# A new order of all pieces in a fused retention and channel-mix kernel: first loads, k's queue, the weights' place

## The chip, the cores and the metric

The kernel runs on one core of a Trainium2 chip. Its engines each work through a queue of their own: TensorE (PE; its weight loads are shown as PEld), VectorE (DVE), ScalarE (ACT), GpSimd (POOL) and SyncE (SP). Transfers are issued by SP, ACT or POOL and carried by 16 DMA engines. The metric is the time of one execution in microseconds (us); before the change it is 160.89 us, the median of 3 runs.

## The reference

Two layers follow each other. The first is a retention recurrence over 4 batches, 8 heads, 768 tokens and 64 channels per head:

```python
for t in range(S):
    state = gamma * state + einsum('bhd,bhe->bhde', k[:, :, t], v[:, :, t])
    y[:, :, t] = scale * einsum('bhd,bhde->bhe', q[:, :, t], state)
```

Its output, turned to 4 x 768 rows of 512 channels, goes into a channel mix:

```python
x_prev = x shifted by one token
xk = mu_k * x + (1 - mu_k) * x_prev
xr = mu_r * x + (1 - mu_r) * x_prev
k = maximum(xk @ w_k, 0)            # 512 -> 1024
v = k * k @ w_v                     # 1024 -> 512
out = sigmoid(xr @ w_r) * v         # 512 -> 512
```

## The kernel before

The recurrence is computed in chunks. Tokens are cut into 12 blocks of 256 tokens, three per batch; a block is two chunks (u = 0, 1) of 128. Scores within a chunk, masked by a triangle, give one part of y; the decayed state handed on from chunk to chunk gives the other. Three weights (w_k, w_v, w_r) stay in SBUF as 16-bit floats.

No loop sets the order. A string `ORDER` lists some 610 words, each one piece of work; a loop at the end of the kernel emits them one by one, and every engine executes its own pieces in this order, waiting where a semaphore says so. A word is a code and its arguments, such as `K.2.1` for the second quarter of the keys of block 2. After `@` stand the PSUM banks (0 to 7) that the piece writes. A piece that takes over a bank waits until its last reader is done. The codes:

| code | engine | what |
|---|---|---|
| lq, lk, lv | POOL; SP for k (POOL with `.2` after the block) | load q, k, v of a block; `lk.n.e.j0.j1` and, after the change, `lq.n.j0.j1` load some head pairs only |
| wk, wr, wv | POOL | load a half of w_k, all of w_r, a half of w_v |
| ks | DVE (`.0`) or POOL (`.1`) | scale k by powers of gamma (L188) |
| T, Tk / Tq | PE | turn scaled k: T in 8 transposes of 128 x 128 (L203), Tk in 32 of 64 x 64 (L221) / turn q in 32 (L221) |
| E | ACT | copy a turned q or k out of PSUM (L249) |
| S, M | PE, DVE | scores (L257) of half i, masked (L264) |
| C, U, G | PE, DVE, POOL | k times v of a block (L282), summed to the state (L294, L298), decayed for the next chunk (L301) |
| I, Y | PE | state part and score part of y (L313, L326) |
| D (Du: of one chunk) | DVE | y scaled by powers of gamma into xT (L340, L348) |
| gy | DVE | builds those powers, in eight small steps (L500, L503) |
| dx (du) | DVE (`.0`) or POOL (`.1`) | x minus the x of the token before (L355) |
| X (Xu) | DVE | xk (`X.n.0`) or xr (`X.n.1`) of one of four channel groups (L369) |
| K, Q (Ku, Qu) | PE, ACT | a quarter of the keys (L406), relu and square (L413, L416) |
| R, s | PE, ACT | gate of 128 tokens (L420), sigmoid (L426) |
| V, O, st | PE, DVE, SP | half of the values product of 128 tokens (L432), times the gate (L438), store (L445) |
| z | PE | products with a tile of zeros (L494), as many as the number says |
| mu, mt, me | ACT, PE, ACT | load, turn and copy mu |

The buffers are rings: 4 for q, v and k as loaded, 3 for scaled k, for turned q and k, for masked scores and for xk and xr, 2 for dx, 5 for results on their way out. q, v and the weights change type on their way in (32 to 16 bits) and are all issued from POOL. At most eight transfers of POOL's queue are under way at once: a ninth waits for the first (the issue of the first half of wv, the tenth, waited for v0), and what stands behind it on POOL waits too.

Of the kernel before, what the change touches and what calls it, by code (L numbers as in the profile page):

```python
# [21 lines left out]
Xu.0.0.1.2.3 Xu.0.0.0.3.4 Xu.0.0.1.1.2 z.9@7 S.1.0@23 lv.3 Xu.0.0.1.3.4 I.1.0@45 Xu.0.0.0.0.1
S.1.1@67 M.1.0 Ku.0.1.1@0 Xu.0.1.0.0.1 Ku.0.0.1@2 Qu.0.1.1 Xu.0.1.0.2.3 Xu.0.0.0.1.2 Xu.0.1.0.3.4
lq.3 Xu.0.0.0.2.3 Qu.0.0.1 Xu.0.1.0.1.2 z.1@3 Ku.0.0.0@0 M.1.1 R.0.0@2 Qu.0.0.0 lk.4.2 ks.2.0 Y.1
U.1.1 lk.6 T.2.1@3 D.1 G.1.1 Ku.0.1.0@1 lv.4 Xu.0.1.1.3.4 V.0.1.0@0 dx.1.0 Qu.0.1.0 V.0.0.0@1 lq.4
Xu.0.1.1.2.3 s.0.0 X.1.0.3.4 R.0.1@4 E.2.1 X.1.0.2.3 X.1.0.1.2 X.1.0.0.1 Tq.2@67 s.0.1 C.2@3
X.1.1.3.4 lq.6 E.2.0 K.1.2@2 X.1.1.0.1 X.1.1.1.2 K.1.3@4 X.1.1.2.3 Q.1.2 U.2.0 G.2.0 K.1.1@5 Q.1.3
ks.3.1 S.2.0@23 I.2.0@67 M.2.0 K.1.0@4 lk.5.2 V.0.0.1 Q.1.0 lv.5 S.2.1@23 T.3.1@4 M.2.1 V.0.1.1
E.3.1 O.0.0 Y.2 Q.1.1 O.0.1 st.0.0 C.3@23 D.2 Tq.3@45 st.0.1 ks.6.1 R.1.0@0 E.3.0 U.3.0 V.1.0.0@1
U.3.1 s.1.0 G.3.1 S.3.0@23 I.3.0@45 S.3.1@67 ks.4.1 R.1.1@0 M.3.1 V.1.0.1 s.1.1 M.3.0 dx.2.1  # L30
T.4.1@0 V.1.1.0@6 O.1.0 E.4.1 st.1.0 Y.3 lk.7 lq.5 X.2.0.3.4 Tq.4@01 X.2.0.2.3 C.4@23 E.4.0
X.2.0.1.2 lv.7 V.1.1.1 X.2.0.0.1 X.2.1.2.3 lv.6 K.2.1@7 X.2.1.1.2 X.2.1.3.4 X.2.1.0.1 K.2.3@0
Q.2.1 U.4.0 D.3 G.4.0 R.2.0@7 Q.2.3 ks.5.1 K.2.0@2 U.4.1 O.1.1 s.2.0 K.2.2@3 Q.2.0 st.1.1 G.4.1
lk.10 S.4.0@67 lk.8 I.4.0@45 Q.2.2 dx.3.1 S.4.1@01 lk.9 V.2.1.0@2 M.4.1 V.2.0.0@3 M.4.0 lq.8
R.2.1@0 X.3.0.2.3 lq.7 V.2.0.1 X.3.0.1.2 s.2.1 X.3.1.0.1 V.2.1.1 X.3.1.1.2 X.3.0.0.1 X.3.1.3.4
C.5@0 Tq.5@67 X.3.0.3.4 Y.4 E.5.0 X.3.1.2.3 O.2.0 T.5.1@1 U.5.0 K.3.0@6 st.2.0 E.5.1 D.4 G.5.0
K.3.1@3 Q.3.0 O.2.1 dx.4.1 S.5.0@45 I.5.0@67 st.2.1 Q.3.1 S.5.1@01 M.5.0 K.3.3@2 M.5.1 K.3.2@3
R.3.0@4 X.4.0.3.4 Q.3.2 X.4.1.2.3 Y.5 X.4.0.0.1 Q.3.3 X.4.1.3.4 Tq.6@01 X.4.1.1.2 C.6@23 X.4.0.1.2
lq.10 E.6.0 V.3.0.0@5 U.6.0 X.4.0.2.3 D.5 T.6.1@2 R.3.1@0 E.6.1 X.4.1.0.1 V.3.0.1 U.6.1 s.3.1
G.6.1 s.3.0 S.6.0@23 I.6.0@01 ks.7.1 S.6.1@67 O.3.0 K.4.0@4 M.6.1 st.3.0 K.4.2@5 dx.5.1 M.6.0  # L40
T.7.1@6 V.3.1.0@7 E.7.1 K.4.3@2 lv.8 X.5.0.0.1 Q.4.0 X.5.1.0.1 K.4.1@6 X.5.0.1.2 Q.4.3 X.5.1.1.2
X.5.0.2.3 V.3.1.1 X.5.1.3.4 Q.4.2 C.7@23 O.3.1 Y.6 Q.4.1 U.7.0 Tq.7@45 D.6 G.7.0 R.4.1@2 E.7.0
ks.8.1 U.7.1 V.4.0.0@6 s.4.1 S.7.0@45 I.7.0@23 S.7.1@01 M.7.0 dx.6.1 V.4.0.1 M.7.1 R.4.0@7 lq.9
Tq.8@45 s.4.0 X.5.0.3.4 C.8@0 X.6.0.1.2 Y.7 E.8.0 lv.9 X.6.1.1.2 O.4.0 T.8.1@7 lv.10 K.5.3@1 D.7
st.4.0 E.8.1 st.3.1 K.5.2@6 lk.11 X.6.1.0.1 X.6.0.2.3 K.5.1@7 X.6.0.3.4 X.6.0.0.1 K.5.0@2
X.6.1.2.3 Q.5.1 X.5.1.2.3 K.6.2@7 dx.7.1 Q.5.2 V.4.1.0@3 Q.5.0 R.5.1@6 lv.11 X.7.1.1.2 Q.6.2
X.7.1.0.1 V.4.1.1 X.6.1.3.4 lq.11 X.7.1.3.4 s.5.1 K.6.1@7 Q.5.3 V.5.1.0@6 R.6.0@1 G.7.1 ks.9.1
U.8.0 K.6.0@2 s.6.0 O.4.1 V.5.1.1 st.4.1 Q.6.0 G.8.0 R.5.0@2 O.5.1 Q.6.1 X.7.0.2.3 st.5.1 S.8.0@01
I.8.0@67 S.8.1@45 M.8.0 s.5.0 V.5.0.0@3 X.7.0.3.4 T.9.1@2 M.8.1 V.5.0.1 E.9.1 V.6.0.0@0 O.5.0
X.7.0.0.1 K.6.3@1 st.5.0 X.7.0.1.2 X.7.1.2.3 Tq.9@23 Q.6.3 Y.8 C.9@45 E.9.0 D.8 R.6.1@1 V.6.0.1  # L50
U.9.0 dx.8.1 s.6.1 U.9.1 S.9.0@67 O.6.0 I.9.0@45 S.9.1@23 K.7.3@1 M.9.0 ks.10.1 R.7.0@0 Q.7.3
K.7.0@1 X.8.0.1.2 K.7.1@6 M.9.1 G.9.1 Q.7.0 R.7.1@1 X.8.1.3.4 s.7.0 X.8.0.2.3 Q.7.1 X.8.0.3.4
Tq.10@23 Y.9 X.8.0.0.1 X.8.1.2.3 C.10@67 s.7.1 T.10.1@0 E.10.0 U.10.0 K.7.2@1 G.10.0 ks.11.1
U.10.1 V.6.1.0@2 D.9 Q.7.2 V.7.0.0@1 E.10.1 G.10.1 V.7.0.1 dx.9.1 V.6.1.1 O.7.0 st.7.0 S.10.0@45
O.6.1 I.10.0@01 S.10.1@67 M.10.0 T.11.1@3 st.6.1 K.8.0@2 M.10.1 K.8.2@4 Q.8.0 X.9.0.3.4 C.11@2
Tq.11@67 E.11.1 X.9.0.2.3 Y.10 X.8.1.0.1 X.8.1.1.2 E.11.0 V.7.1.0@5 X.9.0.1.2 X.9.1.0.1 Q.8.2
V.7.1.1 X.9.0.0.1 U.11.0 D.10 K.8.3@4 G.11.0 K.8.1@2 O.7.1 Q.8.3 dx.10.1 S.11.0@01 I.11.0@45 Q.8.1
S.11.1@67 M.11.0 K.9.0@3 X.9.1.1.2 K.9.3@2 Q.9.0 X.10.1.0.1 X.9.1.2.3 R.8.0@3 M.11.1 V.8.1.0@0
X.9.1.3.4 X.10.1.2.3 Y.11 X.10.0.3.4 X.10.1.1.2 K.9.1@1 D.11 K.9.2@6 dx.11.1 R.8.1@7 Q.9.2 V.8.1.1
Q.9.3 X.11.0.2.3 V.8.0.0@6 X.11.0.1.2 s.8.0 X.10.0.2.3 V.8.0.1 Q.9.1 X.10.0.0.1 X.10.0.1.2 R.9.0@1  # L60
X.11.0.0.1 X.11.1.1.2 K.10.0@3 X.10.1.3.4 s.9.0 X.11.1.3.4 s.8.1 V.9.0.0@1 O.8.0 X.11.0.3.4 st.8.0
R.10.0@2 X.11.1.0.1 st.6.0 st.7.1 K.10.2@6 s.10.0 V.9.1.0@2 R.9.1@7 V.9.1.1 s.9.1 O.8.1 Q.10.2
K.11.1@7 O.9.1 st.8.1 K.11.2@6 X.11.1.2.3 Q.11.1 K.10.3@7 Q.10.0 R.11.1@0 Q.10.3 K.10.1@3 V.9.0.1
# [7 lines left out]
def kernel(  # L71
# [123 lines left out]
    def turned(n, a, j0=0):  # L195
        return banks("T", n, a, j0).bitcast(F16)
# [14 lines left out]
                            Q16(n)[:, 2 * j + hp, i * D : i * D + D], ident,  # L211
                        )

    def trans_small(n, a):
        pt = turned(n, a)[:, :, 0 : 2 * NJ * D].rearrange("p u (j i t) -> p u j i t", j=NJ, i=2)
        for j in range(NJ):
            for i in range(2):
                for u in range(2):
                    r = slice(u * D, u * D + D)
                    for hp in range(2):  # L220
                        nc.tensor.transpose(  # L221
                            pt[hp * D : hp * D + D, u, j, i, :],
                            KS(n)[r, i, 2 * j + hp] if a
                            else Q16(n)[r, 2 * j + hp, i * D : i * D + D], ident[r, r],
                        )
# [346 lines left out]
```

## Time and profile before

| what | value |
|---|---|
| median of 3 runs | 160.89 us (160.67 to 161.34) |
| the profiled execution | 161.76 us, its span 159.5 us |
| PE busy | 151.9 us (95%) |
| DVE busy | 116.7 us (73%) |
| ACT busy | 93.6 us (59%) |
| POOL busy | 75.1 us (47%) |
| moved by the core's transfers | 21.98 MB |
| granted TensorE clock | full in every slice |

The span is the stretch that the profiler records; the execution's own time is 2.3 us more. Busy time is work of an engine, waiting left out. For TensorE the products with zeros count as busy, and so do the first matmuls at the slow pace at which they begin: the first ten products with zeros took 4.45 us, later ones 0.22 to 0.25 us each. A group row names line, engine, operation, out<-in with shapes, the count, then busy us, mean ns of one, and the idle time of the engine just before it with what ended it. Some rows that the steps rest on:

```profile
L432 PE MATMUL ps<-wv,k 128*128 128x512 f16 x184 | 45.2, 379 | 0.1
L406 PE MATMUL ps<-xk,wk 128*128 128x256 f16 x352 | 42.6, 273 | 0.1
...
L494 PE MATMUL ps<-zero 128*128 128x512 f16 x37 | 11.5, 451 | 1.2 <-DVE xT L478 1.2
```

The mean of a matmul is the length of one; since they overlap in the array, eight key matmuls follow each other in 0.87 us and four of 512 columns in 0.86 us.

### The profile page before, as it was taken

What the parts mean: (1) busy time and instruction counts of PE and PEld (TensorE: products, weight loads), DVE (VectorE), ACT (ScalarE), POOL (GpSimd) and SP (SyncE); (2) the same over time, 40 slices, a digit from 0 to 9 for tenths busy, and PEclk for the clock granted to TensorE, in tenths of its full rate; (3) what the DMA queues carried; (4) which work ended last, traced back from release to release, by engine and by line L of the source; (5) the groups of instructions that cost most, each with busy time, mean ns of one, the idle gap of its engine ahead of it and who ended that gap; (6) DMA issues with size and microseconds to landing.
All of it is one profiled execution on the core that took longest, in us unless ns stands there. A gap on an engine that the chain in (4) does not pass through costs nothing.

```text
span 159.5 us, 5601 instructions
## 1 busy us (share of the span) xinstructions
PE 151.9 (95%) x2478; PEld 98.8 (62%) x2478; DVE 116.7 (73%) x209; ACT 93.6 (59%) x148; POOL 75.1 (47%) x73
## 2 busy tenths in 40 slices
PE   7899999998999999999999989999999999999991
...
DVE  0759999849695999978795979797698959431141
...
DMA  5999999999999999475159991100030000510153
GB/s 140 163 246 205 228 245 239 229 222 223 293 209 207 264 244 252 91 128 53 16 60 229 230 147 66 70 6 4 0 132 4 4 0 0 197 70 18 48 197 132
DMA packets 39543, 21.98 MB, mean 138 GB/s; under 512 B 25816, under 2 KB 35936, under 8 KB 39520
## 3 DMA queue, kind: packets, MB, share of 16 engines
...
q14 instruction: 4, 0.03, 0.1%
...
## 4 chain that ended last, share of the span: by engine, by line
PE 65%; DMA 18%; DVE 7%; POOL 5%; issue 2%; POOLq 0%; DVEq 0%
PE ps L432 21%; PE ps L406 19%; PE ps L420 11%; DMA q<-in_q_dram 10%; DMA wk<-in_moe_w_k_dram 8%; DVE xr L369 4%; PE ps L257 3%; PE ps L326 3%; PE ps L203 2%; PE ps L313 2%; POOL v L175 2%; PE ps L221 2%; PE ps L282 1%; DVE xk L369 1%; POOL q L175 1%
## 5 line engine op out<-in xcount | busy, mean ns | idle before, releaser
L432 PE MATMUL ps<-wv,k 128*128 128x512 f16 x184 | 45.2, 379 | 0.1
L406 PE MATMUL ps<-xk,wk 128*128 128x256 f16 x352 | 42.6, 273 | 0.1
L406 PEld LDWEIGHTS <-wk 128*128 128x128 f16 x352 | 33.9, 98 | 7.3
L413 ACT ACTIVATE kr<-ps 128x512 f32<-128x512 f32 x44 | 25.9, 590 | 19.9 <-PE ps L406 19.9
L264 DVE TENSOR_TENSOR a<-ps,c_sb 128x1024 f16<-128x1024 f32 (+1 forms) x26 | 28.9, 1135 | 10.6 <-PE ps L257 9.4
L416 ACT ACTIVATE k<-kr 128x512 f16<-128x512 f32 x44 | 27.7, 630 | 1.4
L432 PEld LDWEIGHTS <-k 128*128 128x128 f16 x184 | 17.3, 98 | 17.8 <-issue 0.2
L355 POOL TENSOR_TENSOR dx<-xT 128x1024 f32<-128x1024 f32 x10 | 18.9, 1890 | 19.1 <-DVE xT L340 15.7
L438 DVE SCALAR_TENSOR_TENSOR os<-ps,rs 128x512 f32<-128x512 f32 x23 | 15.6, 685 | 16.8 <-PE ps L432 9.5
L369 DVE SCALAR_TENSOR_TENSOR xr<-dx,mu,xT 128x256 f16<-128x256 f32 (+1 forms) x52 | 25.3, 518 | 2.1 <-POOL dx L355 2.1
L420 PE MATMUL ps<-wr,xr 128*128 128x512 f16 x96 | 24.8, 379 | 0.5 <-DVE xr L369 0.5
L369 DVE SCALAR_TENSOR_TENSOR xk<-dx,mu,xT 128x256 f16<-128x256 f32 (+1 forms) x52 | 22.9, 478 | 3.0 <-POOL dx L355 3.0
L426 ACT ACTIVATE rs<-ps 128x512 f32<-128x512 f32 x24 | 14.0, 591 | 12.2 <-PE ps L420 12.1
L301 POOL TENSOR_TENSOR tg<-t,csm_sb 128x256 f16<-128x256 f32 x16 | 10.0, 623 | 23.4 <-DVE t L298 23.3
L188 POOL TENSOR_TENSOR ks<-k,csm_sb 128x1024 f16<-128x1024 f32 x9 | 17.1, 1898 | 2.1 <-PE ps L282 2.1
L249 ACT COPY kT<-ps 128x1024 f16<-128x1024 f16 (+1 forms) x13 | 12.3, 944 | 9.7 <-PE ps L203 9.4
L249 ACT COPY qT<-ps 128x1024 f16<-128x1024 f16 x12 | 12.1, 1006 | 5.4 <-PE ps L221 5.4
L175 POOL DMA_DIRECT2D q<-in_q_dram x12 | 11.0, 918 | 8.2 <-PE ps L282 4.4
L420 PEld LDWEIGHTS <-xr 128*128 128x128 f16 x96 | 9.0, 98 | 9.4 <-DVE xr L369 1.0
L340 DVE TENSOR_TENSOR xT<-ps,gy_sb 128x1024 f32<-128x1024 f32 x11 | 13.4, 1217 | 1.1 <-PE ps L326 0.9
L494 PE MATMUL ps<-zero 128*128 128x512 f16 x37 | 11.5, 451 | 1.2 <-DVE xT L478 1.2
L175 POOL DMA_DIRECT2D v<-in_v_dram x12 | 10.8, 902 | 2.4 <-DMA wk<-in_moe_w_k_dram 1.1
...
## 6 DMA issues: line engine op xcount, KB each, us to landing
...
k<-in_k_dram SPq DMA_DIRECT2D x6, 512.0 KB, 11.3
...
```

Source lines behind the costliest of these rows:

```text
L175: eng.dma_start(out=d(n)[:, 2 * j0 : 2 * j1], in_=rows(x, n)[:, 2 * j0 : 2 * j1])
L188: (nc.vector, nc.gpsimd)[e].tensor_tensor(out=KS(n)[:, :, h0:h1], in0=K32(n)[:, h0:h1].rearrange("p h (i d) -> p i h d", i=2), in1=gks[:, ...
L249: nc.scalar.copy(out=out, in_=pt)
L264: nc.vector.tensor_tensor(out=A2(n)[:, i, :, j0:j1], in0=pairs(banks("S", n, i, j0))[:, :, j0:j1], in1=causal[:, i, None, None, :].to_broa ...
L355: (nc.vector, nc.gpsimd)[e].tensor_tensor(out=DX(n)[:, j0:j1, t0:t1], in0=x[:, j0:j1, c + t0 : c + t1], in1=x[:, j0:j1, c - 1 + t0 : c - 1 ...
L369: nc.vector.scalar_tensor_tensor(out=XM[w](n)[:, j, t0:t1], in0=DX(n)[:, j, t0:t1], scalar=mu[:, w * NCO + j : w * NCO + j + 1], in1=x[:, ...
L406: nc.tensor.matmul(pz[:, i, :], lhsT=wk16[:, co, fo * P : fo * P + P], rhs=XM[0](n)[:, co, :], start=(i == 0 and co == 0), stop=(co == NCO ...
L413: nc.scalar.activation(out=kr, in_=banks("K", n, g).rearrange("p (i t) -> p i t", i=2), func=AF.Relu)
L416: nc.scalar.activation(out=K2(n)[:, 2 * g : 2 * g + 2], in_=kr, func=AF.Square)
L420: nc.tensor.matmul(banks("R", n, tb), lhsT=XM[1](n)[:, co, tb * P : tb * P + P], rhs=wr16[:, co, :], start=(co == 0), stop=(co == NCO - 1),)
L432: nc.tensor.matmul(banks("V", n, tb, 0), lhsT=K2(n)[:, fo, tb * P : tb * P + P], rhs=wv16[:, fo, :], start=(fo == 0), stop=(fo == NFO - 1),)
L438: nc.vector.scalar_tensor_tensor(out=OS(2 * n + tb), in0=banks("V", n, tb, 0), scalar=1.0 / (KSC * KSC), in1=RS(2 * n + tb), op0=ALU.mult, ...
```

## The change

The string ORDER is replaced by another one. Beside the order as such, this is different in it:

| | before | after |
|---|---|---|
| first issues on POOL | q0, v0, v1, k1, q1, wk second half, wk first half, wr, k2, wv first half, q2 | q0 (heads 0-3), q0 (heads 4-7), v0, k1, q1, wk first half, wk second half, G.0.1, v1, wv first half, q2, wr, wv second half, k2 |
| k loaded through POOL | blocks 1 to 5 | blocks 1 to 6 and 9 |
| k loaded through SP | 0 (two halves), 6 to 11 | 0 (two halves, in the other order), 7, 8, 10, 11 |
| products with zeros | 37 | 33 |
| turn of k in the small form (Tk) | none | blocks 6, 7, 8, 9, 11 |
| turn and copy of q of block 0 | whole | in two halves of the heads |
| dx on DVE | blocks 0, 1 | blocks 0, 1, 3, 4, 7, 8, 10, 11 |
| ks on DVE | blocks 0, 1, 2 | blocks 0, 1, 2, 9, 10, 11 |
| gy on DVE | behind the two halves of ks of block 0 | ahead of them |

So that q can be turned in halves, three functions take a range of head pairs:

```diff
 ORDER = """
-lk.0.0.2.4 lk.0.0.0.2 lq.0 lv.0 lv.1 lk.1.2 ks.0.0.2.4 lq.1 ks.0.0.0.2 wk.1 gy z.10@1 T.0.1.0.2@0
-T.0.1.2.4@1 E.0.1.0.2 wk.0 mu wr z.4@4 Tq.0@23 E.0.1.2.4 lk.2.2 E.0.0 wv.0 z.5@4 S.0.0.0.2@23
...
+lk.0.0.0.2 lk.0.0.2.4 lq.0.0.2 lq.0.2.4 lv.0 gy lk.1.2 lq.1 wk.0 ks.0.0.2.4 ks.0.0.0.2 wk.1 z.11@1
+T.0.1.0.2@0 T.0.1.2.4@1 E.0.1.0.2 Tq.0.0.2@23 E.0.0.0.2 E.0.1.2.4 z.2@4 S.0.0.0.2@23 Tq.0.2.4@45
+M.0.0.0.2 E.0.0.2.4 mu z.2@6 C.0@01 S.0.0.2.4@45 U.0.0 M.0.0.2.4 z.1@6 I.0.0@23 S.0.1.0.2@67 U.0.1
+S.0.1.2.4@45 M.0.1.0.2 G.0.1 M.0.1.2.4 lv.1 ks.1.0 z.5@0 Y.0 wv.0 Tq.1@45 Du.0.0 lq.2 z.1@0
+T.1.1@6 du.0.0.0 mt@2 wr me Du.0.1 E.1.0 wv.1 Xu.0.0.0.1.2 Xu.0.0.0.3.4 E.1.1 Xu.0.0.0.2.3 lk.2.2
+Xu.0.0.0.0.1 du.0.0.1 Xu.0.1.0.1.2 Xu.0.0.1.3.4 z.11@0 Ku.0.1.0@6 Xu.0.0.1.1.2 Xu.0.1.0.3.4
+Xu.0.0.1.0.1 Ku.0.0.0@7 Xu.0.1.1.1.2 Qu.0.1.0 Xu.0.0.1.2.3 Xu.0.1.1.0.1 C.1@45 Qu.0.0.0 Ku.0.0.1@6
+U.1.0 G.1.0 Qu.0.0.1 U.1.1 S.1.0@23 I.1.0@01 G.1.1 S.1.1@45 M.1.0 V.0.0.0@6 lv.2 M.1.1 V.0.1.0@7
+lk.3.2 Tq.2@23 Xu.0.1.1.2.3 lk.4.2 Xu.0.1.0.0.1 Y.1 Xu.0.1.0.2.3 Xu.0.1.1.3.4 lv.3 Ku.0.1.1@4 D.1
+lq.3 R.0.1@5 Qu.0.1.1 dx.1.0 lk.5.2 R.0.0@4 X.1.0.2.3 lq.4 V.0.0.1 s.0.0 X.1.0.0.1 s.0.1 X.1.0.3.4
+V.0.1.1 X.1.0.1.2 E.2.0 X.1.1.1.2 lv.4 K.1.2@5 ks.2.0 K.1.1@4 Q.1.2 X.1.1.0.1 X.1.1.3.4 C.2@5
+X.1.1.2.3 Q.1.1 T.2.1@2 O.0.0 K.1.0@4 U.2.0 E.2.1 O.0.1 G.2.0 R.1.0@5 Q.1.0 ks.3.1 S.2.0@23
+I.2.0@67 S.2.1@01 M.2.0 s.1.0 K.1.3@4 ks.4.1 lk.7 M.2.1 R.1.1@5 Q.1.3 T.3.1@4 C.3@01 E.3.1 Y.2
+U.3.0 U.3.1 s.1.1 Tq.3@23 D.2 G.3.1 T.4.1@4 E.3.0 V.1.0.0@5 E.4.1 dx.2.1 S.3.0@67 I.3.0@23
+S.3.1@01 M.3.0 V.1.1.0@4 ks.5.1 M.3.1 V.1.0.1 V.1.1.1 O.1.0 lv.5 X.2.0.3.4 Tq.4@01 X.2.0.2.3 Y.3
+X.2.0.0.1 lv.6 X.2.0.1.2 T.5.1@5 D.3 lk.6.2 K.2.1@6 E.5.1 K.2.0@7 lq.5 dx.3.0 Q.2.1 K.2.2@5 lq.6
+Q.2.0 X.2.1.2.3 X.3.0.2.3 K.2.3@6 lv.7 X.3.0.0.1 Q.2.2 X.2.1.3.4 V.2.0.0@7 lq.8 X.3.0.3.4
+X.3.0.1.2 E.4.0 C.4@23 lk.9.2 X.2.1.0.1 X.2.1.1.2 K.3.0@5 Q.2.3 X.3.1.2.3 lq.7 X.3.1.3.4 R.2.0@6
+Q.3.0 X.3.1.1.2 X.3.1.0.1 K.3.1@0 U.4.0 s.2.0 O.1.1 G.4.0 V.2.0.1 Q.3.1 ks.7.1 U.4.1 S.4.0@01
...
-    def trans_small(n, a):
-        pt = turned(n, a)[:, :, 0 : 2 * NJ * D].rearrange("p u (j i t) -> p u j i t", j=NJ, i=2)
-        for j in range(NJ):
+    def trans_small(n, a, j0, j1):
+        pt = turned(n, a, j0)[:, :, 0 : 2 * NJ * D].rearrange("p u (j i t) -> p u j i t", j=NJ, i=2)
+        for j in range(j0, j1):
...
-    def trans_q(n):
-        trans_small(n, 0)
+    def trans_q(n, j0=0, j1=NJ):
+        trans_small(n, 0, j0, j1)
...
     def trans_k(n):
-        trans_small(n, 1)
+        trans_small(n, 1, 0, NJ)
...
-                pt = pt.rearrange("c u (j i p) -> c u j p i", j=NJ, i=2)
-                out = QT(n).rearrange("c j u (p i) -> c u j p i", i=2)
+                pt = pt.rearrange("c u (j i p) -> c u j p i", j=NJ, i=2)[:, :, j0:j1]
+                out = QT(n)[:, j0:j1].rearrange("c j u (p i) -> c u j p i", i=2)
```

The loop that reads ORDER also takes the first head pair of a `Tq` word into the key under which its banks are kept.

More of the change, by code (lines that the diff above doesn't have):

```diff
@@ L16 @@
 ORDER = """
-lk.0.0.2.4 lk.0.0.0.2 lq.0 lv.0 lv.1 lk.1.2 ks.0.0.2.4 lq.1 ks.0.0.0.2 wk.1 gy z.10@1 T.0.1.0.2@0
-T.0.1.2.4@1 E.0.1.0.2 wk.0 mu wr z.4@4 Tq.0@23 E.0.1.2.4 lk.2.2 E.0.0 wv.0 z.5@4 S.0.0.0.2@23
-S.0.0.2.4@01 C.0@45 M.0.0.0.2 U.0.0 lq.2 M.0.0.2.4 z.2@6 I.0.0@23 S.0.1.0.2@67 U.0.1 S.0.1.2.4@01
-M.0.1.0.2 G.0.1 M.0.1.2.4 ks.1.0 z.5@4 Y.0 Du.0.0 z.1@4 C.1@01 mt@6 U.1.0 T.1.1@2 Du.0.1 G.1.0 me
-Tq.1@45 lv.2 du.0.0.1 du.0.0.0 E.1.0 lk.3.2 Xu.0.1.1.1.2 Xu.0.1.1.0.1 E.1.1 Xu.0.0.1.0.1 wv.1
@@ L22 @@
[L22 to L63, printed above, removed]
@@ L64 @@
-Q.10.1 K.11.0@7 O.9.0 Q.11.2 V.10.1.0@3 st.9.0 Q.11.0 V.10.1.1 s.11.1 R.10.1@2 V.10.0.0@0 s.10.1
-V.10.0.1 K.11.3@2 O.10.0 O.10.1 R.11.0@7 st.10.0 Q.11.3 st.9.1 st.10.1 V.11.0.0@6 s.11.0 V.11.0.1
-Vc.11.1.0@7 O.11.0 Vc.11.1.1@2 st.11.0 Oc.11.1.0 sc.11.1.0.0 Oc.11.1.1 sc.11.1.1.1
+lk.0.0.0.2 lk.0.0.2.4 lq.0.0.2 lq.0.2.4 lv.0 gy lk.1.2 lq.1 wk.0 ks.0.0.2.4 ks.0.0.0.2 wk.1 z.11@1
+T.0.1.0.2@0 T.0.1.2.4@1 E.0.1.0.2 Tq.0.0.2@23 E.0.0.0.2 E.0.1.2.4 z.2@4 S.0.0.0.2@23 Tq.0.2.4@45
+M.0.0.0.2 E.0.0.2.4 mu z.2@6 C.0@01 S.0.0.2.4@45 U.0.0 M.0.0.2.4 z.1@6 I.0.0@23 S.0.1.0.2@67 U.0.1
@@ new lines @@
+X.2.0.0.1 lv.6 X.2.0.1.2 T.5.1@5 D.3 lk.6.2 K.2.1@6 E.5.1 K.2.0@7 lq.5 dx.3.0 Q.2.1 K.2.2@5 lq.6
+Q.2.0 X.2.1.2.3 X.3.0.2.3 K.2.3@6 lv.7 X.3.0.0.1 Q.2.2 X.2.1.3.4 V.2.0.0@7 lq.8 X.3.0.3.4
+X.3.0.1.2 E.4.0 C.4@23 lk.9.2 X.2.1.0.1 X.2.1.1.2 K.3.0@5 Q.2.3 X.3.1.2.3 lq.7 X.3.1.3.4 R.2.0@6
+Q.3.0 X.3.1.1.2 X.3.1.0.1 K.3.1@0 U.4.0 s.2.0 O.1.1 G.4.0 V.2.0.1 Q.3.1 ks.7.1 U.4.1 S.4.0@01
+O.2.0 I.4.0@23 S.4.1@45 M.4.0 K.3.3@6 G.4.1 lk.11 R.3.0@7 lk.8 Q.3.3 M.4.1 ks.6.1 st.1.1 st.0.1
+C.5@6 Tq.5@01 st.0.0 U.5.0 Tk.7@45 E.5.0 Y.4 G.5.0 lk.10 R.2.1@6 st.1.0 D.4 s.3.0 lv.8 E.7.1
@@ new lines @@
+V.2.1.0@7 dx.4.0 s.2.1 R.3.1@4 X.4.1.2.3 K.3.2@6 X.4.0.0.1 X.4.0.2.3 V.2.1.1 Q.3.2 X.4.0.3.4
+X.4.1.3.4 V.3.0.0@6 O.2.1 s.3.1 C.6@23 Tk.6@45 U.6.0 S.5.0@01 E.6.1 V.3.1.0@7 U.6.1 M.5.0 G.6.1
+I.5.0@23 ks.8.1 S.5.1@45 V.3.1.1 M.5.1 V.3.0.1 O.3.1 X.4.0.1.2 Tq.6@45 Y.5 O.3.0 E.6.0 K.4.2@7 D.5
+S.6.0@45 Q.4.2 I.6.0@01 S.6.1@23 dx.5.1 M.6.0 K.4.3@6 M.6.1 K.4.1@7 Q.4.3 lq.10 K.4.0@6 X.4.1.1.2
+Q.4.1 X.4.1.0.1 Tq.7@23 X.5.0.3.4 Y.6 Q.4.0 X.5.0.0.1 X.5.0.2.3 C.7@45 lv.10 X.5.1.0.1 R.4.0@6
+E.7.0 X.5.0.1.2 X.5.1.2.3 lq.9 V.4.0.0@7 ks.9.0 s.4.0 lv.9 R.4.1@6 X.5.1.1.2 X.5.1.3.4 K.5.2@2
```

29 lines of the change are left out of this document (28 added, 1 removed).

## The prediction

> **What bounds the kernel now.** I read the page's slices first, then the kernel cut at the one late wait of TensorE, then the chain of waits, then the rows that give the price of a piece.
>
> ```profile
> PE   7899999998999999999999989999999999999991
> DVE  0759999849695999978795979797698959431141
> DMA  5999999999999999475159991100030000510153
> ```
>
> Forty slices of 4 us, each digit a busy share in tenths. The transfers are full from slice 2 to slice 16 (4 to 64 us) and then rare; TensorE looks full throughout. The first part of that is partly show: 37 products with a tile of zeros (11.5 us, by their row) fill waits.
>
> ```profile
> 0.00:38.27 38.27, 34.66 (x631) 21.40 (x632) 28.83 (x64) 19.14 (x29) 23.96 (x32) 1.00 1.31 215
> 38.27:156.20 117.93, 117.27 (x1848) 77.39 (x1848) 87.48 (x146) 74.42 (x119) 51.18 (x42) 1.00 0.59 113
> 156.20:159.50 3.30, 0.00 (x0) 0.00 (x0) 0.41 (x1) 0.00 (x0) 0.00 (x0) 1.00 0.41 143
> ```
>
> The span cut in three: after the stretch and its length come the busy times of PE, PEld, DVE, ACT and POOL, then the granted clock (1.00 throughout), DMA share and GB/s. Up to 38.27 us TensorE is idle 3.6 us and spends 11.5 us on zeros: 15.1 us are no work. From 38.27 to 156.20 us it is idle 0.66 us of 117.93. So the second stretch is bound by TensorE's own work, the first by arrivals; the last is the final store.
>
> ```profile
> 6.53 12.81 DMA wk<-in_moe_w_k_dram
> ...
> 22.17 16.05 DMA q<-in_q_dram
> 38.27 0.44 PE ps L221 x32
> 38.71 0.97 PE ps L420 x4
> 39.68 0.86 PE ps L432 x4
> ```
>
> The chain of waits (start, length, what) says which arrivals: the second half of wk, at 19.3 us, then q of block 3, at 38.2 us. From there it is nearly all matmuls. Prices: a gate (R, L420) or half of a values product (V, L432) costs 0.87 us.
>
> **Arrivals in the new order.** Issue time plus time to landing gives what landed when (us): q0 7.95, v0 9.4, v1 10.9, k1 12.5, q1 13.7, wk second half 16.7, wk first half 19.3, wr 21.9, k2 23.4, wv first half 25.6, q2 27.1, v2 28.6, k3 30.2, wv second half 33.7, v3 36.7, q3 38.2. It is one stream: about 1.5 us for each q, k or v, 2.2 to 3.0 for half a weight; 3.0 to 3.5 where k6 from SP's queue (issued at 24.6, landed at 35.9) shares the engines.
>
> The changed POOL order is q0 (two halves), v0, k1, q1, wk first, wk second, the decay G.0.1, v1, wv first, q2, wr, wv second, k2, G.1.0, G.1.1, v2, k3, k4, v3, q3, k5. Up to the second half of wk it moves the same less v1: 19.3 - 1.5 = 17.8 us. The extra issue costs POOL 0.9 us, hidden because landings trail issues by over 6 us already. Then v1 19.3, wv first 21.5 (+2.2), q2 23.0, wr 25.6 (+2.6). By the second half of wv, before had also moved k2, v2, k3 and some 1.0 us of k6: 33.7 - 1.5 - 1.5 - 1.6 - 1.0 = 28.1. Then k2 29.6 and v2 31.1. By q3 the set is the same with k4 in place of k6: 38.2.
>
> Each G holds the issues behind it on POOL. G.0.1 needs U.0.1 (VectorE), at about 11.5 us as before, so v1 is issued near 12.5 with wk pending until 17.8. G.1.1 needs C.1, which needs v1: about 22, with wr, wv and k2 still pending. Neither drains the stream.
>
> **TensorE in the new order.** The start: the seven small `gy` steps (2.0 us) now stand ahead of the scaling of k0 on VectorE, which therefore ends 0.8 us later than the 5.83 us of before (constants landed at 0.74 + 2.5 = 3.2, `gy` to 5.3, two halves to 6.6); halved q0 wins that back, since the scores of two head pairs start after half a copy (0.59 us, as the half kT copy has, not 1.01). None of it is on the path: wk decides. From 17.8:
>
> - two Ku (0.9 each) to 19.6; C.1 0.4 to 20.0; Ku 0.9 to 20.9; S, I, S of block 1 0.8 to 21.7
> - two V of block 0 (wv there at 21.5) to 23.4; Tq.2, Y.1 1.0 to 24.4; last Ku to 25.3
> - two R from 25.6 (wr) to 27.4; two V from 28.1 (wv) to 29.9
> - two K of block 1 1.75 to 31.6; C.2, T.2, K 1.7 to 33.3; R, S, I, S 1.7 to 35.0; K, R 1.75 to 36.8; T.3, C.3, Y.2 1.4 to **38.2**, and Tq.3 with q3 at 38.2.
>
> Tq.3 thus starts when it did before, but by then R.1.0 and R.1.1 are done, which before followed it; everything else ahead of Tq.3 is the same set. That is 2 x 0.865 = **1.73 us** of work moved into time that was idle or zeros. The four zeros fewer lie in the same interval and are not counted again.
>
> The tight spot is k2, 6 us later than before: its scaling on VectorE (1.15 us, to 30.8) stands ahead of three X (1.2), O (0.6) and U.2.0 (0.34), so 33.1; R.1.0 needs U.2.0's PSUM bank at 33.3. Any lateness of k2 over 0.2 us shows in full.
>
> **The rest of the order.** Five key transposes become the small form (32 instead of 8): the chain has 0.45 or 0.55 us for eight, 0.38 or 0.44 for 32. 5 x 0.08 = **0.4 us** less.
>
> VectorE takes six more differences (blocks 3, 4, 7, 8, 10, 11) and three more scalings (9, 10, 11) from POOL.
>
> ```profile
> L355 POOL TENSOR_TENSOR dx<-xT 128x1024 f32<-128x1024 f32 x10 | 18.9, 1890 | 19.1 <-DVE xT L340 15.7 <-DVE xr L369 3.4
> ...
> L355 DVE TENSOR_TENSOR dx<-xT 128x1024 f32<-128x1024 f32 x1 | 1.2, 1219 | 0.0
> ```
>
> The same operation (busy, mean ns, idle before): 1.89 us on POOL, 1.22 on VectorE, 1.13 to 1.15 when pipelined. Nine cost VectorE 10.2 us. Between 40 and 136 us it is busy 80.4 of 96; 90.6 would be 94%. Walking each block's Y, D, dx, X, K in the new order, X comes before K by at least 0.3 us, except K.3.0 (0.2) and K.2.1 (0.1: S.3.0 ends at 40.4, then two M 2.3, O 0.6, four X 1.6, so 44.9; K.2.1 at 45.0). So I charge nothing here, and the rival below prices it.
>
> Here a rule is weighed. In before, while POOL decays and scales k10 (89.75 to 92.23), four X take 4.90 us where others take 1.66:
>
> ```profile
> 88.02 4.90 DVE L369 SCALAR_TENSOR_TENSOR xr<-dx,mu,xT 128x256 f16<-128x256 f32 x4 [2.08 <-POOL dx L355]
> ...
> 90.32 1.91 POOL L188 TENSOR_TENSOR ks<-k,csm_sb 128x1024 f16<-128x1024 f32 x1
> ```
>
> The Trainium skill (SBUF — State Buffer, "SBUF: two separate sides") says that a VectorE operation with two SBUF inputs and a GpSimd operation that reads SBUF share a port pair and lock each other out for a whole instruction. By the rows, X lost 44 x (550 - 476) + 44 x (502 - 476) ns = 4.4 us to this. Nine of POOL's 19 long operations leave: by the rule VectorE wins back some 9/19, 2.1 us, so its added load is 8.1 us rather than the 10.2 of the plain rows. I take neither as time on the path; only a 0.47 us idle of TensorE at 92.58 came from such a lock.
>
> A second rule speaks against the change: DMA: Bandwidth & Descriptors, "Issuing engine by pattern", sends plain loads to SP. The rows agree on the price: 0.90 us of POOL per issue against 0.41 on SP. The words "all later blocks" hold only in part: k of 1 to 6 and 9 go through POOL (before: 1 to 5), and 7, 8, 10, 11 stay with SP. So two issues, 1.8 us of POOL, by the rule lost; by the trace hidden, since POOL sheds 17 us of long operations. The stretch to watch is the row of nine issues ahead of G.4.0 (free near 51.3, needed at 52.2).
>
> ScalarE has one bad stretch: from the end of T.5.1 it must do two copies, five relu-squares, a sigmoid and a relu (2 x 0.95 + 5 x 1.16 + 0.55 + 0.6 = 8.9 us) before S.4.0 gets its bank; TensorE has six K, two V, an R and a C there, about 8.4. **Cost 0.5 us**; bounds 0 and 1.0 (one more collision of this kind).
>
> SP: lk.11 waits for k7's scaling (about 54.5) ahead of the stores of blocks 0 and 1. Five output buffers cover that: O.2.1, the first to need one back, runs near 62. At the end, the last full stores come 1 us later; stores land in 2.3 us, so up to 0.2 us, in the range.
>
> **Sum.** -1.73 - 0.4 + 0.5 = -1.6 us: span 159.5 to 157.9. The profiled run took 161.76, its span is 159.5, and the median of the runs is 160.89; the difference applied to the median gives **159.3**.
>
> **Rivals.**
> 1. *The stream slips* (nothing gained). If every weight half takes the 3.0 us of the slowest unshared one, wk first half apart, the last wv lands 0.4 + 0.8 + 0.4 + 0.5 = 2.1 us later, and TensorE shifts with it: -1.6 + 2.1 = +0.5, 161.4. For it: k2 has 0.2 us of slack. Against: the total by 38.2 us is measured.
> 2. *VectorE becomes the bound* (slower). At 94% between 40 and 136 us, D, dx, X queue behind M and O. If from block 3 on each of nine blocks costs TensorE 0.4 us, 3.6 us: -1.6 + 3.6 = +2.0, **162.9**. It decides once more than 0.18 us per block is lost. For it: dx and M in one queue. Against: the freed port, and VectorE idle 11.6 of the last 16 us before 152.
> 3. *More gain*: the ScalarE stretch is absorbed, the idle at 92.58 goes, three weight halves take 2.4 rather than 2.6 us: -2.1 - 0.5 - 0.6, 157.7.
>
> **How the numbers follow.** Forecast 0.54, stream slips 0.19, VectorE bound 0.19, more gain 0.08. A measurement of this kernel tells 0.5%, 0.8 us, from no change (160.1 to 161.7). Faster: 0.50 of the forecast and 0.08, 0.58 in all. Slower: the VectorE case and 0.03 of a slipped stream, 0.22. Same: 0.20. Range 157.7 to 162.0; the forecast's own is 158.2 to 160.3.
>
> **What would show it.** Right: the second half of wk at about 17.8, of wv at 28; Tq.3 near 38.2 with R.1.0 and R.1.1 ahead of it; TensorE's idle after that below 1.5 us. Wrong: TensorE waiting in the middle for xk, xr or a (VectorE) by more than 2 us in sum; wv past 30; an idle gap at S.4.0 far from 0.5.

## The result, and the profile after

The changed kernel takes **164.89 us** (median of 4 runs, 164.79 to 167.02) beside 161.12 us for the kernel before on the same chip: a ratio of 1.026, 95% interval 1.0219 to 1.0300. It is slower by 3.8 us where 1.6 us of gain were forecast, and lies outside the range of 157.7 to 162.0. The profiled execution took 167.02 us, the longest of the four, with a span of 165.2 us and a mean clock of 0.976; the others have spans of 163.0 to 163.1 and a clock of 0.99, so the lost times read below are those of the worst of the four. Medians in this document are of all executions of a kernel, while the ratios and intervals leave out those over 1.5% above the kernel's fastest (five of e2's 22, and one each of e3, e4, e5 and e9; e5's, at 300.5 us, is the one that was profiled, so its trace is not used). In this trace, and in those of e2, e3 and e9, a line of the code stands one higher than in the listing (L433 is its L432).

The slices of its page, in tenths, with the clock that TensorE was granted:

```profile
PE   7799999999999999099999999999999999999991
DVE  3649988967899875267998997799879898911351
PEclk9999999999999999758999999999999999999998
```

A hole is in TensorE's row at slice 16, counted from 0 (66 to 70 us), and one in VectorE's row beside it. Right behind the hole the clock falls to half. No slice of the kernel before has either. The list of TensorE's waits gives the hole in one row (engine and line, what it waited for, us in total, times, longest):

```profile
PE ps L433 <- DVE os L439: 3.9, 1, 3.9
```

The chain of waits says what VectorE waited for (start, length, what):

```profile
60.90 0.61 SPq L446
...
61.56 0.43 SPq L446
...
62.04 6.97 DMA out_dram<-os
...
69.13 0.70 DVE os L439
...
69.88 1.86 PE ps L433 x4
```

V.3.1.0 (L433) may not write PSUM bank 7 before O.2.1 (L439) has read it. O.2.1 writes the sixth result, so it needs back the first of the five output buffers, and the store st.0.0 that empties this one was issued only at 62.04 and landed at 69.0. O.2.1 itself sat idle on VectorE for 4.87 us, so it was there at 64.26 (69.13 - 4.87). The result of st.0.0 had been ready for over 20 us. SyncE's timeline (start, length, what) shows what the store stood behind:

```profile
36.53 21.03 SPq L176 DMA_DIRECT2D k<-in_k_dram  x3
57.61 4.91 SPq L446 DMA_DIRECT2D out_dram<-os  x3
62.63 1.38 SPq L176 DMA_DIRECT2D k<-in_k_dram  x1
```

k7 went out at 36.53; the next on the queue, k11, waited for its buffer until GpSimd had scaled k7, at 56.5. Then k11 (56.56), k8 (57.11) and st.1.1 (57.61) were issued, and the issue of st.1.1 alone took 3.91 us, so that st.0.1 and st.0.0 came at 61.56 and 62.04. The chain begins this issue at 60.90 only because VectorE's D.4 ended then, and the list of waits puts 3.3 us of it down to D.4; but in the kernel st.1.1 needs only O.1.1, done at 54.6, and loads of k took as long to issue where they stood third in a row (4.02 us in the kernel before, 5.90 in e1).

The stretches around the hole (after the stretch and its length: busy PE, PEld, DVE, ACT, POOL; then clock, DMA share, GB/s):

```profile
66.00:68.00 2.00, 0.01 (x1) 0.03 (x1) 0.00 (x0) 0.86 (x1) 0.00 (x0) 1.00 1.15 350
68.00:70.00 2.00, 0.12 (x1) 0.10 (x1) 0.87 (x2) 0.00 (x0) 0.00 (x0) 0.60 0.94 282
70.00:72.00 2.00, 2.00 (x16) 0.62 (x17) 1.71 (x3) 0.00 (x0) 1.22 (x2) 0.50 0.14 50
72.00:74.00 2.00, 2.00 (x26) 1.00 (x21) 1.14 (x1) 0.00 (x0) 1.24 (x1) 0.50 0.00 0
74.00:76.00 2.00, 2.00 (x37) 0.75 (x37) 1.32 (x4) 0.00 (x0) 0.00 (x0) 0.69 0.00 0
```

While TensorE stands, the transfers run at 350 GB/s. When it goes on, it does so at half the clock for some 5 us: 1.0 + 1.0 + 0.6 = 2.6 us of work lost at most, beside 3.87 us of idle. The Trainium skill (TensorE: Matmul & The Clock Gate, "What's actually happening") says that an idle window of about 3.4 us throttles TensorE and that about 3.4 us of steady work free it again; the idle here fits, the way back took longer (work from 69.88, full clock from about 75.2).

Elsewhere the trace is as quiet as forecast: from Tq.3 on, no other wait of TensorE reaches 0.5 us.

### The profile page after: what moved, and what is told of

It is laid out like the page before. It is cut to its first block, busy times and chain, and to the rows that moved or that the text cites. A ratio compares the mean times of both kernels' runs of the same rounds, so it can differ in the third digit from the quotient of the medians.

```text
span 165.2 us, 5822 instructions
## 1 busy us (share of the span) xinstructions
PE 154.6 (94%) x2594; PEld 99.0 (60%) x2594; DVE 124.5 (75%) x218; ACT 93.6 (57%) x149; POOL 60.6 (37%) x67
## 4 chain that ended last, share of the span: by engine, by line
PE 70%; DMA 12%; ACT 6%; DVE 3%; POOL 2%; issue 1%; SPq 1%; DVEq 0%
PE ps L433 22%; PE ps L407 20%; PE ps L421 10%; DMA wv<-in_moe_w_v_dram 8%; DMA out_dram<-os 4%; PE ps L258 4%; PE ps L327 3%; PE ps L222 3%; PE ps L314 2%; PE ps L204 2%; ACT kr L414 2%; ACT k L417 2%; PE ps L283 2%; ACT qT L250 1%; PE ps L451 1%; PE ps L495 1%
## 5 line engine op out<-in xcount | busy, mean ns | idle before, releaser
L433 PE MATMUL ps<-wv,k 128*128 128x512 f16 x184 | 46.8, 393 | 4.1 <-DVE os L439 3.9
L407 PE MATMUL ps<-xk,wk 128*128 128x256 f16 x352 | 43.4, 273 | 0.0
L433 PEld LDWEIGHTS <-k 128*128 128x128 f16 x184 | 17.9, 100 | 23.3 <-issue 6.7
L439 DVE SCALAR_TENSOR_TENSOR os<-ps,rs 128x512 f32<-128x512 f32 x23 | 15.7, 688 | 18.5 <-PE ps L433 5.4
L421 PE MATMUL ps<-wr,xr 128*128 128x512 f16 x96 | 24.0, 379 | 0.3 <-ACT rs L427 0.2
L370 DVE SCALAR_TENSOR_TENSOR xr<-dx,mu,xT 128x256 f16<-128x256 f32 (+1 forms) x52 | 22.1, 459 | 0.1
L370 DVE SCALAR_TENSOR_TENSOR xk<-dx,mu,xT 128x256 f16<-128x256 f32 (+1 forms) x52 | 21.8, 459 | 0.0
L250 ACT COPY qT<-ps 128x1024 f16<-128x1024 f16 (+1 forms) x13 | 12.3, 944 | 12.1 <-PE ps L222 12.0
L176 POOL DMA_DIRECT2D q<-in_q_dram x13 | 11.7, 906 | 2.6 <-DMA wv<-in_moe_w_v_dram 1.8
L258 PE MATMUL ps<-qT,kT 64*64 64x128 f16 x384 | 11.9, 227 | 0.1
L189 POOL TENSOR_TENSOR ks<-k,csm_sb 128x1024 f16<-128x1024 f32 x6 | 11.3, 1895 | 0.0
## 6 DMA issues: line engine op xcount, KB each, us to landing
k<-in_k_dram POOLq DMA_DIRECT2D x7, 512.0 KB, 10.3
```

Of the source, the lines that this page charges most:

```text
L176: eng.dma_start(out=d(n)[:, 2 * j0 : 2 * j1], in_=rows(x, n)[:, 2 * j0 : 2 * j1])
L258: nc.tensor.matmul(pa[u * D : u * D + D, hp, j, :], lhsT=KT(n)[r, j, i, u * D : u * D + D], rhs=QT(n)[r, j, u, :], start=(j == j0), stop=( ...
L370: nc.vector.scalar_tensor_tensor(out=XM[w](n)[:, j, t0:t1], in0=DX(n)[:, j, t0:t1], scalar=mu[:, w * NCO + j : w * NCO + j + 1], in1=x[:, ...
L407: nc.tensor.matmul(pz[:, i, :], lhsT=wk16[:, co, fo * P : fo * P + P], rhs=XM[0](n)[:, co, :], start=(i == 0 and co == 0), stop=(co == NCO ...
L421: nc.tensor.matmul(banks("R", n, tb), lhsT=XM[1](n)[:, co, tb * P : tb * P + P], rhs=wr16[:, co, :], start=(co == 0), stop=(co == NCO - 1),)
L433: nc.tensor.matmul(banks("V", n, tb, 0), lhsT=K2(n)[:, fo, tb * P : tb * P + P], rhs=wv16[:, fo, :], start=(fo == 0), stop=(fo == NFO - 1),)
```

## The experiments

The expectations of e1 to e4 weigh theory S (the whole loss is one wait, for the stores of blocks 0 and 1 that are held behind loads of k, and the slow clock after it) against rival L (the new order is slower by itself). From e5 on, theory A adds to S a delay of TensorE's instructions; its rivals are B (the second stop belongs to TensorE's order) and C (VectorE, with nine more operations, is the bound). All edits but e4's start from the changed kernel; words are those of ORDER.

**e1, the stores ahead of the loads.**

```diff
-... G.4.1 lk.11 R.3.0@7 lk.8 Q.3.3 ... st.1.1 st.0.1 ... st.0.0 ... lk.10 R.2.1@6 st.1.0
+... G.4.1 R.3.0@7 Q.3.3 ... st.1.1 st.0.1 ... st.0.0 st.1.0 lk.8 lk.11 ... lk.10 R.2.1@6
```

> The changed kernel with four words moved: the stores of blocks 0 and 1 stand ahead of the loads of k8 and k11 on SyncE's queue. Theory S (the whole loss is one wait: the result O.2.1 needs the output buffer of the first store, which stands behind k11 and k8; 3.9 us of idle TensorE, and then 1.6 to 3.3 us at half clock): 160.3 us, 0.995 of before, no idle of TensorE over 1 us past 30 us, granted clock 1.00 there. Rival L (the new order is slower by itself, VectorE's added differences and scalings; the wait only stands where the lag shows): 162.5 or more, with the idle moved to later pieces.

Measured: 163.79 us, ratio 1.0174 (1.0151 to 1.0197). The wait for the output buffer is gone, but only 1.1 us came back. TensorE's waits show another in its place, inside Y.5, which ends with nothing that the profile shows:

```profile
PE ps L313 <- issue: 2.4, 1, 2.4
```

It lasts from 68.74 to 71.15 us, and behind it the clock is again at half (0.50 from 72 to 74 us). So held stores were a cause, not the only one. The time alone would fit rival L; e6 and e10, which keep the order of all the computing engines, rule it out below.

**e2, eight output buffers, order untouched.**

```diff
-    OS = ring("os_", 5, [dm], F32)
+    OS = ring("os_", 8, [dm], F32)
```

> The changed kernel with 8 output buffers for 5, its order untouched: the stores go as late as before, but no result waits for one. Theory S: 160.3 us, like the moved stores. If the lateness of the stores itself mattered (their traffic beside the loads of q, k and v), it would stay above 162; rival L: 162.5 or more.

Measured: 161.14 us, ratio 0.9997 (0.9982 to 1.0013). That is 0.8 us more than theory S expected. The stores are as late as ever, but nobody needs their buffers. The wait without a releaser stands at the same place, shorter (68.56 to 70.16), and in this execution the clock stays whole. The chain around it:

```profile
68.12 0.38 PE ps L222 x32
68.50 0.06 PE ps L314 x2
68.56 1.60 issue
70.16 0.24 PE ps L314 x2
```

**e3, work without use in the hole.** Twelve products with zeros (`z.12@4`) ahead of V.3.1.0, so that TensorE isn't idle long enough for the clock to fall.

> The changed kernel with 12 products of zeros (2.6 us) put ahead of the piece that waits, so that TensorE is idle about 1 us there instead of 3.9. They shift nothing else, since the wait ends when the store lands. Theory S splits the loss into idle and clock: this takes away the clock's part, 164.9 - 1.6 = 163.3 us, granted clock 1.00. If the half clock cost nothing (waits for other engines there anyway): 164.9, the same as the changed kernel.

Measured: 163.92 us, ratio 1.0188 (1.0150 to 1.0225), the clock 1.00 in every slice. Some 1 us of the loss is the clock, then, and the rest the wait; the interval just meets that of the changed kernel (1.0219 to 1.0300), so the 1 us is rough.

**e4, the converse.** The kernel before, with its first store moved behind the load of k9.

```diff
-... O.0.0 Y.2 Q.1.1 O.0.1 st.0.0 C.3@23 ...
+... O.0.0 Y.2 Q.1.1 O.0.1 C.3@23 ... lk.9 st.0.0 ...
```

> The kernel before with one word moved: the first store stands behind the loads of k10, k8 and k9 on SyncE's queue. Theory S: the store lands at about 65, O.2.1 wants its buffer at 59.5, TensorE stands for some 5 us and then runs at half clock: 166 to 169 us. Rival L (it is the new order): one late store is covered by the other four buffers: 161 to 162.

Measured: 167.88 us, ratio 1.0398 (1.0346 to 1.0451). TensorE waits 4.0 us for an output (`os`), and the clock falls to 0.988 on the mean. One store behind the loads of k is enough.

**What the wait in Y.5 is.** In the view of the transfer queues cut into quarters of a microsecond, a queue called "instruction" moves one packet of 16 KB every 3 to 16 us. In e1 such packets lie near 61.5 and 68.75, in e2 near 61.0 and 67.75; in the three runs below that lack the stall (e6, e9, e10) near 61.25 to 61.75 and again at 65.25 to 66.0. The gap is 4.0 to 4.25 us there and 6.75 to 7.25 in e1 and e2, so their second packet is 2.5 to 3 us late, while k8, k11, k10 and the stores are moved. It is not the rate alone: 238 GB/s in e1 from 61.6 to 68.8 us, and 231 in e6 from 61.9 to 66.1, where the packet was on time. What differs is SyncE's queue (q1), here its packets, MB and share of the engines in these stretches of e1 and then e6 (86% in e2, 52 to 57% in e9 and e10):

```profile
q1 hardware_dynamic: 2424, 1.30, 76.9%
q1 hardware_dynamic: 1073, 0.60, 53.9%
```

TensorE stops at the same count. From the packet to the stop, e1 and then e2 (columns as in the stretches above):

```profile
61.60:68.74 7.14, 7.14 (x165) 3.85 (x163) 6.49 (x12) 2.73 (x4) 1.99 (x2) 1.00 1.33 237
```

```profile
61.10:68.56 7.46, 7.46 (x167) 4.13 (x166) 6.77 (x13) 2.73 (x4) 2.47 (x2) 1.00 1.20 296
```

165 and 167 matmuls with 163 and 166 weight loads; in e6 the next packet was there after 101. The reading: TensorE runs out of instructions because their next packet came late.

Shorter stops of the same kind, in the middle of a piece and with no releaser, stand in other traces. The rows from the start to such a stop, of the kernel before, the changed one, e10 and e2 (the counts in brackets are the matmuls, then the weight loads):

```profile
0.00:15.90 15.90, 13.69 (x223) 6.84 (x223) 9.34 (x27) 3.84 (x6) 10.73 (x17) 1.00 1.22 188
0.00:24.70 24.70, 22.27 (x349) 12.18 (x350) 17.34 (x45) 9.18 (x15) 14.74 (x23) 1.00 1.25 188
0.00:43.90 43.90, 40.18 (x733) 24.63 (x733) 34.17 (x71) 21.84 (x34) 29.09 (x35) 1.00 1.29 219
0.00:68.60 68.60, 64.75 (x1244) 40.57 (x1245) 56.22 (x109) 37.76 (x60) 45.41 (x51) 1.00 1.28 217
```

That is 446, 699, 1,466 (also in e6, e7, e8 and e11) and 2,489 instructions (also in e1): 253, 767 and 1,023 apart, which is 1, 3 and 4 times 256 to within three. A trace of the changed kernel has 20 such packets for 5,188 matmuls and weight loads, some 260 to a packet. So TensorE stops where a packet ends; and in all nine traces with such a stop (those over 0.2 us; 0.27 to 2.41 us long) it goes on 2.25 to 2.6 us after the start of the next packet. The stop belongs to the packet, whatever piece it falls in. The next two runs take the three loads apart.

**e5 and e6, the loads spread.** e5 issues each store behind its result (`O.0.0 st.0.0` and so on), and both move the loads:

```diff
-... ks.4.1 lk.7 ... lk.11 R.3.0@7 lk.8 ... lk.10 R.2.1@6 ... lq.10 ... st.2.1
+... ks.4.1 lk.7 lk.8 ... R.3.0@7 ... R.2.1@6 ... lk.10 lq.10 ... st.2.1 lk.11
```

e6 leaves the stores where the change has them and has eight output buffers, so it differs from e2 by the loads alone.

> The changed kernel, with the four stores of blocks 0 and 1 issued right behind their results, k8 behind k7, and k10 and k11 moved to where their buffers have long been free (about 75 and 95 us). Theory A (both stalls near 66 to 70 us come from SyncE's queue: the stores held behind the k loads, and TensorE's instruction fetch delayed while k8, k11, k10 and the stores are moved at once): no wait of TensorE over 0.8 us between 60 and 75 us, granted clock 1.00 there, 159.0 to 160.3 us, faster than before by 0.4 to 1.2 per cent. Rival B (the wait without a releaser in Y.5 belongs to the order on TensorE, not to the transfers): a wait of 1 to 2.4 us stays near 68 us, 161 to 163.5 us. Rival C (VectorE with nine more operations is the bound once the stores are mended): waits for VectorE of over 2 us in sum, 161 us or more.

> Eight output buffers as in e2, stores left where the changed kernel has them, and only the three loads k8, k11, k10 taken apart as in e5. Theory A: the stall of 1.6 us in Y.5 that e2 showed falls to the usual 0.3 to 0.5 us, and with it the slower group of e2's runs goes: 159.3 to 160.3 us. Rival B: 1.6 us stay, 161 us as in e2.

Measured: e5 160.57 us, ratio 0.9956 (0.9932 to 0.9980); e6 160.14 us, 0.9926 (0.9899 to 0.9954). e5 lies 0.3 us past its expectation's end. In e6's trace no wait of TensorE after 40 us exceeds 0.3 us, and Y.5 has none. Beside e2 the stall and 1 us went with nothing changed but the place of three loads. Rival B (the order of TensorE) falls: that order is the same.

**e7, the nine operations back on GpSimd.** Six `dx.n.0` to `dx.n.1` and three `ks.n.0` to `ks.n.1`, from e5.

> e5, with the nine operations (six differences, three scalings of k) that the change gave to VectorE back on GpSimd, at the same places of the order. My theory (VectorE has room, and GpSimd's port lock costs TensorE little): within 0.5 us of e5, rather slower than faster. Rival C (VectorE is what bounds the changed kernel): 1 us or more faster than e5.

Measured: 163.55 us, ratio 1.0147 (1.0111 to 1.0183): 3 us slower than e5, six times what I allowed for. The groups of e7:

```profile
L369 DVE SCALAR_TENSOR_TENSOR xk<-dx,mu,xT 128x256 f16<-128x256 f32 x44 | 20.9, 513 | 5.4 <-POOL dx L355 5.3
L369 DVE SCALAR_TENSOR_TENSOR xr<-dx,mu,xT 128x256 f16<-128x256 f32 x44 | 20.6, 504 | 4.2 <-POOL dx L355 4.1
```

VectorE waits 9.4 us for differences that take 1.94 us each on GpSimd. Far from binding, VectorE's nine operations are worth 3 us in this order.

**e8, v1 sooner.** `lv.1` ahead of `G.0.1`, from e5.

> e5, with v of block 1 issued ahead of the decay G.0.1 on GpSimd, so 0.5 us sooner. If the stream of loads on GpSimd's queue is thinned by the late issue of its next transfers: wv's second half lands 0.4 us sooner, and the time falls by 0.2 to 0.5 us from e5. If the stream is bound by how fast it is moved: no difference above 0.2 us.

Measured: 160.32 us, ratio 0.9939 (0.9915 to 0.9964), within the scatter of e5; the 0.25 us between them are little more than the 0.2 that divide the two expectations. The first half of wv was issued at 11.36 us (14.06 in the changed kernel, 12.23 in e6, 12.87 in e10), and the second half landed at 28.15, between e10's 27.37 and the changed kernel's 28.94. So the landing scatters by more than this edit could win; what binds the stream is not decided.

**e9, a burst where there was none.** e6 with three loads that nobody needs (k8, k9, k10 again, into free buffers) behind st.3.1.

> e6, the quickest so far, with three loads of 512 KB each (k8, k9, k10 once more, into buffers that nobody reads any longer) put on SyncE's queue behind the store st.3.1, at about 93 to 95 us, where e6 moves 4 to 5 GB/s from 96 to 104 us. Nothing waits for them. Theory A (a burst on SyncE's queue delays TensorE's instruction packets): the packet that e6 has at 99.0 us comes 1 to 3 us later, and TensorE stands 0.5 to 2.4 us without a releaser between 98 and 104 us; the time rises by 0.5 to 2.5 us. Rival B (the stall near 68 us belongs to what stands there): no stall, the time of e6.

Measured: 159.71 us, ratio 0.9903 (0.9876 to 0.9929): no loss. Half of the expectation held. The burst moved 334 GB/s (96 to 98 us) and the packet came at 100.75 us instead of 99.0. But no stall followed, and the count says why. From the packet at 94.5 to the late one, and from the start to 2.3 us behind the late one:

```profile
94.60:100.85 6.25, 6.25 (x145) 4.76 (x144) 5.25 (x7) 3.28 (x6) 0.00 (x0) 1.00 1.07 275
0.00:103.10 103.10, 98.27 (x1938) 64.71 (x1939) 87.87 (x156) 62.39 (x98) 54.55 (x60) 1.00 1.08 190
```

This packet is the sixth behind the one that Y.5 waited for, so it is wanted at about instruction 4,025 (2,489 + 6 x 256, an estimate from the stops). When it could be used, TensorE was at 3,877 (1,938 + 1,939), so no stop was due. Long matmuls stand there (17 from 100 to 102 us), where short ones use the instructions up in e1 (93 from 64 to 66 us). That a burst on SyncE's queue delays a packet is shown by this one place and by e1 and e2; I made no new stop with it.

**e10, one word.** The smallest mend: k11 goes out behind st.2.1, and nothing else is changed. k8 then waits only for block 4's scaling and leaves near 37 us.

```diff
-... G.4.1 lk.11 R.3.0@7 lk.8 ... st.4.1 Tk.8@67 st.2.1 E.9.1
+... G.4.1 R.3.0@7 lk.8 ... st.4.1 Tk.8@67 st.2.1 lk.11 E.9.1
```

> The changed kernel with one word moved: k11 from ahead of the stores of blocks 0 and 1 to behind the store st.2.1 (about 87 us). k8 waits only for block 4's scaling and so goes out near 38 us, the stores when their results are there. Theory A: both waits near 66 to 70 us go, 160.1 to 161.0 us, as e5. If the held stores were not the cause: 163 us and more.

Measured: **159.83 us**, ratio 0.9912 (0.9886 to 0.9939): quicker than both kernels, and 0.3 us below what I expected. SyncE's timeline, to lay beside the changed kernel's:

```profile
0.74 36.87 SPq L175 DMA_DIRECT2D k<-in_k_dram  x4
53.82 2.22 SPq L445 DMA_DIRECT2D out_dram<-os  x3
58.21 0.39 SPq L175 DMA_DIRECT2D k<-in_k_dram  x1
```

Three stores leave by 56 us, each lands in about 7 us, and O.2.1 (63.67) finds its buffer. The page's slices have neither hole nor slow clock (a stop of 0.79 us for instructions, at 43.65, is too short to show):

```profile
PE   6699998999989999999999999999999999999991
PEclk9999999999999999999999999999999999999999
```

**e11, the two small gains together.** e8 with eight output buffers.

> e8 with eight output buffers in place of five, the two small gains together. If the stores of e8 never wait for a buffer any more: the time of e8, 160.0 to 160.4 us. If they still did: up to 0.4 us faster.

Measured: 160.26 us, ratio 0.9937 (0.9913 to 0.9962), the time of e8, so the buffers were no limit there. Among e6, e8, e9, e10 and e11 the intervals overlap; I call none of them the best, and e10 the simplest.

## Why the prediction was wrong

**The step that failed** is the one on SP: "Five output buffers cover that: O.2.1, the first to need one back, runs near 62." It named the right wait and put its cost at nothing, by comparing the wrong times. O.2.1 was due at 64.3, k7 was scaled at 56.5 rather than 54.5; neither is the fault. I let the stores be free at once from then on. Five things lay between: two loads issued, 3.91 us in which st.1.1 could not be issued, two more stores, and 6.97 us until st.0.0 had landed. That last figure was there to be read: in the trace of before, the stores of 30 to 75 us took a median of 7.4 us to land. By my own time for k7, 54.5, with 1.0 us for issuing two loads, 1.0 for three stores and 7.4 to land, the buffer is back at 63.9, already past 62. I had used the 2.3 us of the last stores, when nothing else is moved. The issue that blocks was there to be read as well: in the kernel before, three loads of k in a row took SyncE 5.89 us to issue, 4.02 of it the third, where a load alone takes 0.39.

```profile
50.36 5.89 SPq L175 DMA_DIRECT2D k<-in_k_dram  x3
```

The signs of being wrong that I had named watched VectorE, wv and ScalarE, and did not show the loss: no wait of TensorE for xk, xr or a in the middle, wv at 28.94, ScalarE's idle 0.15 us where 0.5 was set. None watched SyncE's queue.

**The second cost was not in the sum at all.** The same queue then moved three loads of k and the stores at once, and TensorE's instructions came late behind them. e2, with the first cost covered, still lost the whole gain to it (0.9997 beside e6's 0.9926). In the changed kernel itself it lies hidden in the hole: the next packet came at 68.6, while TensorE stood for the store.

**The clock** was taken as 1.00 throughout, as in before. A wait of 3.87 us made that false; by e3 it is some 1 us of the loss. Together the trace accounts for it: from Tq.3 to the last matmul the changed kernel took 122.18 us, e10 116.56, and the 5.6 us between lie within 3.87 of idle and up to 2.6 of slow clock.

**The rest of the sum held in the main, in part by luck.** With one word mended, e10 has a span of 158.1 us in its profiled execution, where 157.9 were forecast from the 159.5 of one execution of before. Over all executions of that comparison the median span is 158.05 in e10 and 159.0 in before, a gain of 0.95 us rather than 1.6. The terms:

- *Two gates ahead of Tq.3, -1.73.* In the changed kernel Tq.3 came at 39.62, so only 0.4 us of it showed (38.27 + 1.73 - 39.62). But it is 38.79 in e6, 38.50 in e8 and 38.11 in e10, with both gates done in each: 1.2 to 1.9 us. The size was right; it is the landing of the stream that scatters, by 1.5 us between executions, which the forecast's range hardly had: the second half of wv landed at 28.94 in the changed kernel, 28.43 in e6, 28.15 in e8 and 27.37 in e10 (28.1 forecast), and Tq.3 followed 10.3 to 10.7 us later in each.
- *The middle, -1.73 - 0.4 + 0.5 from Tq.3 on.* From Tq.3 to the last matmul before took 117.88 us, which makes 116.25; e10 took 116.56. ScalarE's stretch cost 0.15 us of idle at 52 us in both traces, not 0.5; against that, e10 lost 0.79 us to a stop for instructions in Tq.4 that no term had. The small transposes were not measured apart.
- *VectorE's nine operations at nothing.* Right as a cost, and e7 shows a gain of 3 us behind it that I had not seen as one. For X of 256 columns before has means of 550 and 502 ns, the changed kernel 479 in both halves, and e7, with the nine back on GpSimd, 504 and 513. So the nine are worth 44 x 0.025 + 44 x 0.034 = 2.6 us of VectorE's time, near the 2.1 us reckoned from the Trainium skill (SBUF — State Buffer, "SBUF: two separate sides"); the other 1.5 of the 4.1 us against before came with the order. The larger price in e7 is the waiting for differences, 9.4 us where before has 5.1.
- *Issues through POOL, at nothing.* Nothing speaks against it: e8 issued the weights 0.9 to 2.7 us sooner than the changed kernel and the runs that leave v1 in its place, and won nothing that can be told apart.

Of the rivals, rival 1 (the stream slips) shows in part in the 39.62 of one execution; rival 2 (VectorE) had the sign for a reason that e7 rules out, and its 162.9 lay outside my own range; rival 3 (more gain) did not come.
